# Linear attention with a gated feed-forward on one Trainium2 core: keys and outputs turned by VectorE blocks and a round trip through HBM instead of by TensorE

## The chip, the core and the metric

The kernel runs on one core of a Trainium2 chip. The core has five engines with their own instruction queues: TensorE (PE; its weight loads are listed apart as PEld), VectorE (DVE), ScalarE (ACT), GpSimd (POOL) and SyncE (SP), which here issues nearly all DMAs. The metric is the device time of one execution, in microseconds (us).

## What is computed

`y` is a recurrent linear attention over 768 steps for 4 batches and 8 heads of 48; its output, seen as 3072 tokens of 384, goes through a gated feed-forward layer of width 1536. All is float32.

```python
for t in range(S):
    cur = np.einsum('bhd,bhe->bhde', u[None] * kt, vt)
    y[:, :, t] = np.einsum('bhd,bhde->bhe', rt, state + cur)
    state = wt[:, :, :, None] * state + np.einsum('bhd,bhe->bhde', kt, vt)
...
gate = 1.0 / (1.0 + np.exp(-(x @ w_gate)))
val = x @ w_val
return (gate * val @ w_out)
```

## The kernel before

The sequence is cut into 24 pieces of 128 steps, which the code numbers `q`: `q // 4` is the place in the sequence (0 to 5), `q % 4` the batch. The text calls them chunks. Four chunks with the same place in the sequence make a row of 512 tokens, `n = q // 4`, for the feed-forward layer. Its weights are split into 12 blocks `f` of 128 hidden units.

**The order of the work.** Row 0 and the attention of the first chunks are ordered by a small planner (`plan.run()`), which the change doesn't touch. What follows is a loop over rows 1 to 5 and their 12 blocks, 60 steps in all, in an order written out by hand. One step issues on PE: `gate` (9 matmuls of 128x512 into the bank `pg`), `value` (9 into `pu`), and `down` of the step before (9 into `po`). On the other engines follow `sigmoid` (ACT, reads `pg`, writes `sg`), `hidden` (DVE, reads `pu`, writes `sg`), `hidden_hi` (ACT, `hh`) and `hidden_lo` (DVE, `hl`). There is one bank `pg` and one bank `pu`.

**The attention in the loop.** A step has four slots, before `gate`, before `value`, before `down` and after it. The table `todo` holds, for each of the 240 slots, what else is issued there. The attention of chunk q is done at slot `time` of `visit` (7, 19, 31 and 43 in each row of 48 slots, so every 12 slots or three steps). Around it stand:

- `load_pin`, `load_tok` (SP): decay, keys and receptances by lanes (`pin`), and all three by tokens (`tok`), for chunk q + 2.
- `prepare(q + 1)`, a few slots ahead of the visit: `bonus1`, `bonus2` (POOL, products of `tok` into `bon`), `scan_k` and `prep_k` (DVE, a scan into `eg` and the product with the keys), `fade`; `turn_k` (PE, four transposes of 112x128 keys into the bank `turn`) and `take_k` (ACT, three copies to `kT`); `prep_r` (DVE, a scan and a product), `bonus3` (DVE, a sum over `bon`) and `bonus4` (POOL, into `at`).
- `both(q)` (PE): `carry` and `blend` of chunk q into the banks `py` and `pz`, `score` and `total` of chunk q + 1 into `pa`. `pz` is a tile of the tag `pu`, so it is the same bank as that of `value`. Two steps of this order go through a no-operation on SP (`relay`).
- `take_y` (ACT, two copies into `bon`), and on DVE `mask`, `middle`, `keep` of chunk q + 1.
- `turn_x` (PE, three transposes of `bon`, 128x128, into the bank `turn`), `take_x` (ACT) and `rest_x` (DVE), three slots after the visit: they write chunk q's part of the feed-forward's input `x`.

Tiles of one tag take turns in a fixed number of buffers. `bon` has two, so that of chunk q + 2 is the one of chunk q, and the first writer of the new tile waits for the last reader of the old one.

Of the kernel before, what the change touches and what calls it, by code (L numbers as in the profile page):

```python
# [21 lines left out]
P = 128  # L22
C = 128
# [30 lines left out]
WHEN = [0, 2, 3, 5, 6]  # L54
EARLY = [(0, 3, 4, 4), (11, 16, 16, 16), (23, 26, 28, 28), (35, 38, 40, 40)]
HC = C // 2
# [159 lines left out]
def tile_kernel(ctx: ExitStack, tc: tile.TileContext, dec: bass.AP, tok: bass.AP, wts: bass.AP, u: bass.AP, side: bass.AP, out: bass.AP):  # L216
# [90 lines left out]
    def load_pin(q):  # L307
        t = p2.tile([P, KW + 2 * NP * C], F32, tag="pin", name=f"pin{q}")
        for i, j in ((0, KW), (KW, KW + 2 * NP * C)) if q == 0 else ((0, KW + 2 * NP * C),):
            nc.sync.dma_start(t[:, i:j], dec[place(q)][:, i:j])  # L310
        pin[q] = t[:L]

# [87 lines left out]

    def take_k(q):
        kT[q] = p1.tile([P, NP * L], F32, tag="kT", name=f"kT{q}")
        if not swapped(q):
            nc.scalar.copy(kT[q], bank["k", q][:, :NP * L])
# [27 lines left out]
    def total(q, p, o, s):  # L432
        m = D if o or swapped(q) else 64
        return nc.tensor.matmul(  # L434
            bank["a", q][64 * o:64 * o + m, s, NP * HC + p * D:NP * HC + (p + 1) * D],
            lhsT=kT[q][rows(q, s, o), p * L + 64 * o:p * L + 64 * o + m], rhs=values(q, p, o, s),
            start=True, stop=True, skip_group_check=True)
# [123 lines left out]
    def take_x(q):  # L561
# [9 lines left out]
        nc.scalar.activation(to[:, :, spot(q)], bank["x", q], AF.Copy, accum_out=acc_x[:, q:q + 1])  # L571

# [73 lines left out]
    def check_bounds():  # L646
# [181 lines left out]

# [74 lines left out]
```

## Time and profile before

| | |
|---|---|
| time, median of 3 runs | 565.79 us (564.51 to 567.89) |
| the profiled execution: time, span of its instructions | 565.15 us, 563.3 us |
| PE busy (share of the span) | 546.7 us (97%) |
| DVE busy | 329.9 us (59%) |
| ACT busy | 213.6 us (38%) |
| POOL busy | 99.6 us (18%) |
| mean granted TensorE clock, as a share of full speed | 0.997 |

The span runs from the first to the last instruction; the time is 1.85 us longer, for what lies around it. A busy share is a mean over the whole execution: what bounds a stage is read from the waits in it.

### The profile page before, as it was taken

The page shows a single profiled execution, that of the slowest core. Times are in us where ns is not written, and L with a number is a line of the kernel's source. Part 1 is how long each engine was busy: PE and PEld are TensorE (multiplying, and loading weights), DVE is VectorE, ACT ScalarE, POOL GpSimd, SP SyncE. Part 2 cuts the span into 40 slices and gives each one's busy share as a digit, 9 for nine tenths or more (in the row PEclk, how much of TensorE's full clock was granted, in tenths as well). Part 3 has the DMA queues.
Part 4 walks back from the last instruction along what each step waited for, and adds up shares of the span by engine and source line. Part 5 has one row for each costly group of instructions (what it writes and reads, how often), then busy time and mean ns, then how long its engine had stood idle before and what let it go on. Part 6 is the DMA issues. An engine that isn't in the chain of part 4 may idle for free.

```text
span 563.3 us, 12542 instructions
## 1 busy us (share of the span) xinstructions
PE 546.7 (97%) x5487; PEld 451.0 (80%) x5487; DVE 329.9 (59%) x477; ACT 213.6 (38%) x428; POOL 99.6 (18%) x86
## 2 busy tenths in 40 slices
PE   8899899999999999999999999999999999999995
PEld 7788788868788888888888888888888888888883
DVE  5889999897775764664654654654654622321221
ACT  3759544634543333423323422323423232312111
POOL 4453302142022111120210210220320200000000
PEclk9999999999999999999999999999999999999998
DMA  8499123603122032122022122022122000100001
GB/s 318 147 390 420 76 77 128 263 0 113 51 94 101 0 101 99 57 100 99 2 99 100 56 100 99 1 100 97 60 99 99 2 1 1 57 1 1 1 1 62
DMA packets 11570, 51.73 MB, mean 92 GB/s; under 512 B 1393, under 2 KB 1778, under 8 KB 9970
## 3 DMA queue, kind: packets, MB, share of 16 engines
q1 hardware_dynamic: 9346, 46.90, 22.3%
q10 hardware_dynamic: 2160, 3.93, 1.8%
q8 instruction: 45, 0.74, 0.5%
q14 instruction: 19, 0.16, 0.1%
HBM read 46.11 MB, written 4.72 MB: 90 GB/s over the span
## 4 chain that ended last, share of the span: by engine, by line
PE 84%; DVE 5%; DMA 4%; ACT 3%; issue 2%; SPq 1%; POOL 0%; ACTq 0%; DVEq 0%; POOLq 0%
PE po L635 23%; PE pg L592 16%; PE pu L592 15%; PE pu L595 8%; PE pg L595 7%; DMA raw<-wts 4%; PE po L631 2%; PE py L442 2%; PE pa L428 2%; PE pu L589 2%; PE pg L589 2%; PE pk L394 1%; PE pa L434 1%; PE px L551 1%; PE py L448 1%
## 5 line engine op out<-in xcount | busy, mean ns | idle before, releaser
L612 DVE TENSOR_TENSOR sg<-pu,sg 128x512 f32<-128x512 f32 (+2 forms) x78 | 50.6, 649 | 137.5 <-PE pu L595 135.3
L635 PE MATMUL po<-hh,w 128*128 128x512 f32 x402 | 127.7, 399 | 0.4 <-ACT hh L616 0.4
L592 PE MATMUL pg<-x,w 128*128 128x512 f32 x402 | 105.3, 397 | 0.0
L592 PE MATMUL pu<-x,w 128*128 128x512 f32 x402 | 102.5, 390 | 0.0
L605 ACT ACTIVATE sg<-pg 128x512 f32<-128x512 f32 (+2 forms) x78 | 44.0, 564 | 141.2 <-PE pg L595 135.0
L616 ACT CAST hh<-sg 128x512 fp32r<-128x512 f32 x67 | 41.5, 620 | 135.9 <-DVE sg L612 135.9
L592 PEld LDWEIGHTS pu<-x,w 128*128 128x128 f32 x402 | 75.2, 188 | 15.5
L592 PEld LDWEIGHTS pg<-x,w 128*128 128x128 f32 x402 | 73.6, 188 | 16.1 <-issue 0.3
L635 PEld LDWEIGHTS po<-hh,w 128*128 128x128 f32 x402 | 72.9, 188 | 14.3 <-ACT hh L616 0.8
L635 PE MATMUL po<-hl,w 128*128 128x512 f32 x201 | 78.6, 391 | 0.5 <-DVE hl L620 0.5
L620 DVE TENSOR_TENSOR hl<-sg,hh 128x512 fp32r<-128x512 f32 x67 | 50.6, 756 | 41.7 <-ACT hh L616 41.7
L329 POOL TENSOR_TENSOR bon<-tok,ub 128x384 f32<-128x384 f32 x21 | 27.4, 1303 | 208.3 <-DMA tok<-tok 179.3
L595 PE MATMUL pu<-x,w 128*128 128x512 f32 x201 | 56.8, 391 | 0.0
L595 PE MATMUL pg<-x,w 128*128 128x512 f32 x201 | 56.5, 389 | 0.0
L350 POOL TENSOR_TENSOR at<-eye,a 128x512 f32<-128x512 f32 x24 | 33.1, 1380 | 131.1 <-DVE a L336 124.8
L635 PEld LDWEIGHTS po<-hl,w 128*128 128x128 f32 x201 | 37.8, 188 | 9.5 <-DVE hl L620 1.1
L595 PEld LDWEIGHTS pg<-x,w 128*128 128x128 f32 x201 | 37.7, 188 | 8.1
L595 PEld LDWEIGHTS pu<-x,w 128*128 128x128 f32 x201 | 37.7, 188 | 7.9
L357 DVE TENSOR_TENSOR_SCAN eg<-pin,ends 112x516 f32<-112x516 f32 x24 | 34.8, 1450 | 7.1 <-DMA pin<-dec 7.1
L518 DVE COPY_PREDICATED at<-after,pa 128x512 f32<-128x512 int32 x24 | 17.7, 737 | 31.0 <-PE pa L434 27.6
L332 POOL TENSOR_TENSOR bon<-bon,tok 128x384 f32<-128x384 f32 x21 | 32.4, 1543 | 1.6
L377 DVE TENSOR_TENSOR_SCAN eg<-pin,heads 112x516 f32<-112x516 f32 x24 | 29.4, 1226 | 0.0
(94 smaller groups left out, 672.3 us busy)
## 6 DMA issues: line engine op xcount, KB each, us to landing
pin<-dec SPq DMA_DIRECT2D x23, 772.0 KB, 4.6
raw<-wts SPq DMA_DIRECT2D x12, 1152.0 KB, 10.8
tok<-tok SPq DMA_DIRECT2D x21, 576.0 KB, 5.8
y<-o ACTq DMA_DIRECT2D x15, 256.0 KB, 2.0
y<-o SPq DMA_DIRECT2D x3, 256.0 KB, 3.4
tok<-tok SPq DMA_DIRECT2D x3, 192.0 KB, 9.3
pin<-dec SPq DMA_DIRECT2D x1, 512.0 KB, 4.2
pin<-dec SPq DMA_DIRECT2D x1, 260.0 KB, 2.9
```

Source lines behind the costliest of these rows:

```text
L329: nc.gpsimd.tensor_tensor(out=bon[q], in0=tk[q][:, 0:DM], in1=ub, op=ALU.mult)
L332: nc.gpsimd.tensor_tensor(out=bon[q], in0=bon[q], in1=tk[q][:, DM:2 * DM], op=ALU.mult)
L350: engine.tensor_tensor(out=att[q], in0=eye.unsqueeze(1).unsqueeze(1).broadcast_to(shape), in1=a0, op=ALU.mult)
L357: nc.vector.tensor_tensor_scan(out=e[:, 516:0:-1], data0=t[:, 516:0:-1], data1=ends[:, 516:0:-1], initial=0.0, op0=ALU.mult, op1=ALU.add,)
L377: nc.vector.tensor_tensor_scan(out=e[:, WW:WW + 516], data0=t[:, 0:516], data1=heads[:, 0:516], initial=0.0, op0=ALU.mult, op1=ALU.add,)
L592: nc.tensor.matmul(t, lhsT=w[f][:, cols], rhs=x[n][:, a, k, spot], start=k == 0 and j == 0, stop=False)
L595: nc.tensor.matmul(t, lhsT=whi[f][:, cols], rhs=x[n][:, 1, k, i0 * C:i1 * C], start=False, stop=k == NKT - 1)
L605: nc.scalar.activation(sg, hid["g", n, f, i0], AF.Sigmoid)
L612: nc.vector.tensor_tensor(out=sg, in0=hid["u", n, f, i0], in1=sg, op=ALU.mult)
L616: nc.scalar.copy(hh, hid["s", n, f, i0])
L620: nc.vector.tensor_tensor(out=hl, in0=hid["s", n, f, i0], in1=hid["hi", n, f, i0].bitcast(F32), op=ALU.subtract)
L635: nc.tensor.matmul(to, lhsT=w[f][:, cols], rhs=h, start=first and i == 0, stop=last and i == 2, skip_group_check=True)
```

## The change

From chunk 10 on the keys are no longer turned by PE. DVE turns the 32x32 blocks of the key tile within themselves (`nc.vector.transpose` into `near`), one DMA writes the result to HBM (`far`), and four DMAs read it back, each into 32 partitions, in runs of 128 elements, so that the blocks come to their places. `take_k` then copies from `near` instead of from a PSUM bank. In the same way the outputs of the first three chunks of each row are turned: DVE blocks of `bon`, one write of 128x384, four reads in runs of 96 elements back into `bon`. The fourth chunk of a row is still turned by PE. `turn_k` moves to the slot of `prep_k`, eight slots before the visit, and `take_k` stays behind at three before; `turn_x` moves to the visit itself, `take_x` and `rest_x` to eight slots after it. `load_tok` is issued after the new DMAs. The tile `sg` has one buffer instead of two in the loop, to make room.

```diff
+AWAY = 10
...
-EARLY = [(0, 3, 4, 4), (11, 16, 16, 16), (23, 26, 28, 28), (35, 38, 40, 40)]
+EARLY = [(0, 3, 4, 4), (11, 11, 16, 16), (23, 23, 28, 28), (35, 35, 40, 40)]
+Q = 32
+NQ = P // Q
...
+    def away_k(q):
+        return q >= AWAY
+
+    def away_x(q):
+        return swapped(q) and q % B < B - 1
+
     def turn_k(q):
+        if away_k(q):
+            near = stage.tile([P, NP * C], F32, tag="blocks", name=f"bk{q}")
+            nc.vector.transpose(
+                out=near.rearrange("a (j p t) -> a p j t", j=NQ, t=Q),
+                in_=deep[q][:, KW:KW + NP * C].rearrange("a (p j t) -> a p j t", j=NQ, t=Q))
+            far = away.tile([P, NP * C], F32, tag="k", name=f"far_k{q}")
+            nc.sync.dma_start(far, near)
+            of = far.rearrange("(i t) (j w) -> t i j w", t=Q, j=NQ)
+            for j in range(NQ):
+                nc.sync.dma_start(near[j * Q:(j + 1) * Q].rearrange("a (i w) -> a i w", i=NQ), of[:, :, j])
+            bank["k", q] = near
+            return
...
     def take_k(q):
-        kT[q] = p1.tile([P, NP * L], F32, tag="kT", name=f"kT{q}")
+        kT[q] = p1.tile([P, NP * C], F32, tag="kT", name=f"kT{q}")
+        if away_k(q):
+            to = kT[q].rearrange("a (p o i t) -> a o i p t", p=NP, o=2, t=Q)
+            of = bank["k", q].rearrange("a (o i p t) -> a o i p t", o=2, i=2, t=Q)
+            nc.scalar.copy(to[:, 0], of[:, 0])
+            for s, half in enumerate(HALVES):
+                nc.scalar.copy(to[half, 1], of[HALVES[1 - s], 1])
+            return
...
     def turn_x(q):
+        if away_x(q):
+            near = stage.tile([P, NP * C], F32, tag="blocks", name=f"bx{q}")[:, :DM]
+            nc.vector.transpose(
+                out=near.rearrange("a (g k t) -> a k g t", g=NQ, t=Q),
+                in_=bon[q].rearrange("a (k g t) -> a k g t", g=NQ, t=Q))
+            far = away.tile([P, DM], F32, tag="x", name=f"far_x{q}")
+            nc.sync.dma_start(far, near)
...
+            for g in range(NQ):
+                nc.sync.dma_start(to[g * Q:(g + 1) * Q], of[:, :, g])
...
+            return
...
-        sg = hid["s", n, f, i0] = stage.tile([P, (i1 - i0) * C], F32, tag="sg", bufs=2, name=f"sg{n}_{i0}_{f}")
+        sg = hid["s", n, f, i0] = stage.tile([P, (i1 - i0) * C], F32, tag="sg", bufs=1 + (n < R0), name=f"sg{n}_{i0}_{f}")
...
         at(early, prep_k, q)
+        if away_k(q):
+            at(early, turn_k, q)
         at(early, fade, q)
-        at(turn, turn_k, q)
-        at(turn, take_k, q)
+        if away_k(q):
+            at(late, take_k, q)
+        else:
+            at(turn, turn_k, q)
+            at(turn, take_k, q)
...
-            prepare(q + 1, *EARLY[q - start] if q < start + B else (time - 7, time - 5, time - 3, time - 3))
+            prepare(q + 1, *EARLY[q - start] if q < start + B else (time - 8, time - 8, time - 3, time - 3))
         at(time, both, q)
         at(time, take_y, q)
         if q + 1 < NG:
+            at(time, mask, q + 1)
+        if q + 2 < NG:
+            at(time, load_pin, q + 2)
+        if away_x(q):
+            at(time, turn_x, q)
+        if q + 1 < NG:
             settle(q + 1, time)
         if q + 2 < NG:
-            at(time, load, q + 2)
-        at(time + 3, turn_x, q)
-        at(time + 3, take_x, q)
-        at(time + 3, rest_x, q)
+            at(time, load_tok, q + 2)
+        if not away_x(q):
+            at(time + 3, turn_x, q)
+        wait = 8 if away_x(q) else 3
+        at(time + wait, take_x, q)
+        at(time + wait, rest_x, q)
```

The queue of SP around the visit of chunk 13, which loads for chunk 15, before (`pin` and `tok` are the two loads; the number behind a name is its chunk, then the tile's own):

```order
L310 DMA pin14_2788<-dec 128x1544
L316 DMA tok14_2790<-tok 128x1152
L310 DMA pin15_3009<-dec 128x1544
L316 DMA tok15_3011<-tok 128x1152
L310 DMA pin16_3229<-dec 128x1544
```

And now, from the loads of chunk 15 to the next:

```order
L314 DMA pin15_3037<-dec 128x1544
L584 DMA far_x13_3041<-bx13_3039 128x384
L588 DMA bon13_2627<-far_x13_3041 32x4x96 x4
L320 DMA tok15_3052<-tok 128x1152
L408 DMA far_k15_3099<-bk15_3097 128x512
L411 DMA bk15_3097<-far_k15_3099 32x4x128 x4
L314 DMA pin16_3264<-dec 128x1544
```

Between the two loads of a visit stand the write and the four reads of chunk 13's output, and behind them the write and the four reads of chunk 15's keys.

The queue of DVE from the first step after that visit to `hidden` of the third, before (`x` is `rest_x`, `eg` and `pin` are `scan_k` and `prep_k`, then `prep_r`, `a0` is `bonus3`, `sg` is `hidden`, `hl` is `hidden_lo`):

```order
L581 TENSOR_TENSOR x3_2823<-px13_3040,x3_2823 128x3x128
L357 SCALAR_TENSOR_TENSOR eg15_3058<-pin15_3009,ends_77 112x516
L361 RECIPROCAL heads_80<-eg15_3058 112x4
L366 TENSOR_TENSOR pin15_3009<-pin15_3009,eg15_3058 112x512
L372 TENSOR_TENSOR ready15_3062<-state3_105,eg15_3058 112x192
L612 TENSOR_TENSOR sg2_0_6_3074<-pu2_0_6_3076,sg2_0_6_3074 128x512
L620 TENSOR_TENSOR hl2_0_6_3089<-sg2_0_6_3074,hh2_0_6_3087 128x512
L377 SCALAR_TENSOR_TENSOR eg15_3058<-pin15_3009,heads_80 112x516
L382 TENSOR_TENSOR pin15_3009<-pin15_3009,eg15_3058 112x512
L336 TENSOR_REDUCE a015_3111<-bon15_3055 128x8
L612 TENSOR_TENSOR sg2_0_7_3125<-pu2_0_7_3127,sg2_0_7_3125 128x512
```

And now:

```order
L361 SCALAR_TENSOR_TENSOR eg15_3093<-pin15_3037,ends_79 112x516
L365 RECIPROCAL heads_82<-eg15_3093 112x4
L370 TENSOR_TENSOR pin15_3037<-pin15_3037,eg15_3093 112x512
L404 STREAM_TRANSPOSE bk15_3097<-pin15_3037 128x4x4x32
L376 TENSOR_TENSOR ready15_3105<-state3_107,eg15_3093 112x192
L658 TENSOR_TENSOR sg2_0_6_3117<-pu2_0_6_3119,sg2_0_6_3117 128x512
L666 TENSOR_TENSOR hl2_0_6_3132<-sg2_0_6_3117,hh2_0_6_3130 128x512
L626 TENSOR_TENSOR x3_2915<-bon13_2627,x3_2915 128x3x128
L381 SCALAR_TENSOR_TENSOR eg15_3093<-pin15_3037,heads_82 112x516
L386 TENSOR_TENSOR pin15_3037<-pin15_3037,eg15_3093 112x512
L340 TENSOR_REDUCE a015_3151<-bon15_3090 128x8
L658 TENSOR_TENSOR sg2_0_7_3165<-pu2_0_7_3167,sg2_0_7_3165 128x512
```

`rest_x` of chunk 13 has moved from ahead of `scan_k` to behind the second step's `hidden_lo`, and a block transpose of the keys stands behind `prep_k`. The block transpose of chunk 13's output stands ahead of these rows, at the visit, behind `mask`.

The queue of POOL with the semaphores that each instruction waits for, before (`bon` is `bonus1` and `bonus2`, `at` is `bonus4`; each DMAHW name is one of the semaphores of the DMAs):

```order
L329 TENSOR_TENSOR bon14_2835<-tok14_2790,ub_89 128x384 [waits DMAHW2_49,PE_49,Activation_49]
L332 TENSOR_TENSOR bon14_2835<-bon14_2835,tok14_2790 128x384 [waits Pool_49]
L350 TENSOR_TENSOR at14_2893<-eye_84,a014_2891 128x512 [waits DVE_49]
L329 TENSOR_TENSOR bon15_3055<-tok15_3011,ub_89 128x384 [waits DMAHW4_49,PE_49,Activation_49]
L332 TENSOR_TENSOR bon15_3055<-bon15_3055,tok15_3011 128x384 [waits Pool_49]
```

And now:

```order
L333 TENSOR_TENSOR bon14_2862<-tok14_2824,ub_91 128x384 [waits DMAHW2_49,DMAHW6_49,DMAHW1_49,DMAHW7_49,DMAHW0_49,DVE_49]
L336 TENSOR_TENSOR bon14_2862<-bon14_2862,tok14_2824 128x384 [waits Pool_49]
L354 TENSOR_TENSOR at14_2926<-eye_86,a014_2924 128x512 [waits DVE_49,PE_49]
L333 TENSOR_TENSOR bon15_3090<-tok15_3052,ub_91 128x384 [waits DMAHW4_49,DMAHW5_49,DMAHW3_49,DMAHW6_49,DMAHW2_49,DVE_49]
L336 TENSOR_TENSOR bon15_3090<-bon15_3090,tok15_3052 128x384 [waits Pool_49]
```

`bonus1` of chunk 15 waited for PE, which read `bon` of chunk 13 last, in its transposes. It now waits for DVE, whose `rest_x` of chunk 13 reads that buffer last, eight slots after the visit.

## Rows read from the trace of the kernel before

**Rows 1.** Busy time of each engine in a stretch of two rows of tokens:

```profile
242.00:327.00 85.00, 85.00 (x864) 70.20 (x863) 48.18 (x76) 28.29 (x63) 15.98 (x12) 1.00 0.21 74
```

**Rows 2.** Waits of PE from 142 to 560 us: in total, times, longest:

```profile
PE pz L442 <- DVE sg L612: 0.9, 1, 0.9
```

**Rows 3.** Timeline of PE around chunk 13's visit: start, duration, engine, line, instruction:

```profile
259.48 0.25 PE L442 MATMUL py<-mid,pin 48*64 48x48 f32 x1
...
264.92 0.85 PE L595 MATMUL pu<-x,w 128*128 128x512 f32 x3
...
267.81 0.39 PE L635 MATMUL po<-hl,w 128*128 128x512 f32 x1
268.03 1.53 PE L592 MATMUL pg<-x,w 128*128 128x512 f32 x6
...
274.61 1.53 PE L592 MATMUL pg<-x,w 128*128 128x512 f32 x6
...
278.02 0.84 PE L595 MATMUL pu<-x,w 128*128 128x512 f32 x3
...
280.51 0.39 PE L635 MATMUL po<-hl,w 128*128 128x512 f32 x1
```

**Rows 4.** Timeline of PE, two starts of a step without attention:

```profile
505.28 1.52 PE L592 MATMUL pg<-x,w 128*128 128x512 f32 x6
511.40 1.52 PE L592 MATMUL pg<-x,w 128*128 128x512 f32 x6
```

**Rows 5.** Groups of instructions by line and shape: busy us, mean ns of one:

```profile
L394 PE MATMUL pk<-ident,pin 112*128 112x112 f32 x96 | 13.9, 268 | 0.8 <-ACT whole L571 0.7
...
L551 PE MATMUL px<-ident,bon 128*128 128x128 f32 x72 | 11.8, 273 | 0.5 <-ACT a L407 0.5
```

**Rows 6.** Timeline of DVE after that visit:

```profile
267.87 0.55 DVE L581 TENSOR_TENSOR x<-px,x 128x384 fp32r<-128x384 f32 x1
...
276.26 0.55 DVE L336 TENSOR_REDUCE a<-bon 128x8 f32<-128x384 f32 x1
278.97 0.69 DVE L612 TENSOR_TENSOR sg<-pu,sg 128x512 f32<-128x512 f32 x1 [2.16 <-PE pu L595]
```

**Rows 7.** Instructions of tiles `pin`, `tok`, 230 to 470 us: ns minimum/median/maximum:

```profile
L382 DVE TENSOR_TENSOR pin<-pin,eg x11: 691/693/694, 233.0 to 446.4; 112x512 f32<-112x512 f32 x11
...
L357 DVE TENSOR_TENSOR_SCAN eg<-pin,ends x10: 1222/1580/1939, 247.0 to 439.0; 112x516 f32<-112x516 f32 x10
L366 DVE TENSOR_TENSOR pin<-pin,eg x10: 661/1224/1229, 248.4 to 441.1; 112x512 f32<-112x512 f32 x10
...
L329 POOL TENSOR_TENSOR bon<-tok,ub x10: 1012/1028/1917, 247.1 to 438.9; 128x384 f32<-128x384 f32 x10
L332 POOL TENSOR_TENSOR bon<-bon,tok x10: 1342/1816/1824, 249.1 to 440.0; 128x384 f32<-128x384 f32 x10
```

**Rows 8.** DMA issues: line, KB each, median us from issue to landing:

```profile
pin<-dec SPq DMA_DIRECT2D x23, 772.0 KB, 4.6
...
y<-o ACTq DMA_DIRECT2D x15, 256.0 KB, 2.0
...
weigh<-side SPq DMA_DIRECT2D x1, 3.5 KB, 1.7
```

**Rows 9.** Timeline of SP at that visit:

```profile
260.80 0.33 SPq L310 DMA_DIRECT2D pin<-dec  x1
```

**Rows 10.** Timeline of ACT after that visit:

```profile
267.13 0.48 ACT L571 ACTIVATE x<-px 128x384 fp32r<-128x384 f32 x1
...
273.13 0.62 ACT L616 CAST hh<-sg 128x512 fp32r<-128x512 f32 x1 [2.19 <-DVE sg L612]
...
274.03 0.64 ACT L412 COPY kT<-pk 64x192 f32<-64x192 f32 x2
...
276.92 0.60 ACT L605 ACTIVATE sg<-pg 128x512 f32<-128x512 f32 x1 [2.25 <-PE pg L595]
```

**Rows 11.** Groups of instructions of DVE from 142 to 230 us (`w_lo`):

```profile
L299 DVE TENSOR_TENSOR w<-raw,w 128x1152 fp32r<-128x1152 f32 x5 | 7.5, 1491 | 0.0
```

More of the change, by code (lines that the diff above doesn't have):

```diff
@@ L223, in tile_kernel @@
     ps1 = own.enter_context(tc.tile_pool(name="ps1", bufs=1, space=PSUM))
+    away = own.enter_context(tc.tile_pool(name="away", bufs=2, space=bass.MemoryType.DRAM))
     early = tc.tile_pool(name="early", bufs=1)
@@ L299, in w_lo @@
         nc.vector.tensor_tensor(out=wlo[f], in0=full(f), in1=whi[f].bitcast(F32), op=ALU.subtract)
-    pin, tk, eg, bon, kT, att, ready, mid, bank = {}, {}, {}, {}, {}, {}, {}, {}, {}
+    deep, pin, tk, eg, bon, kT, att, ready, mid, bank = {}, {}, {}, {}, {}, {}, {}, {}, {}, {}
     def place(q):
@@ L310, in load_pin @@
             nc.sync.dma_start(t[:, i:j], dec[place(q)][:, i:j])
-        pin[q] = t[:L]
+        pin[q], deep[q] = t[:L], t
     def load_tok(q):
@@ L401, in take_k @@
     def take_k(q):
-        kT[q] = p1.tile([P, NP * L], F32, tag="kT", name=f"kT{q}")
+        kT[q] = p1.tile([P, NP * C], F32, tag="kT", name=f"kT{q}")
[6 more added lines that the diff above has]
+            return
         if not swapped(q):
-            nc.scalar.copy(kT[q], bank["k", q][:, :NP * L])
+            nc.scalar.copy(kT[q][:, :NP * L], bank["k", q][:, :NP * L])
             if q in LANES:
@@ L432, in total @@
     def total(q, p, o, s):
-        m = D if o or swapped(q) else 64
+        m, i = D if o or swapped(q) else 64, p * (C if away_k(q) else L) + 64 * o
         return nc.tensor.matmul(
             bank["a", q][64 * o:64 * o + m, s, NP * HC + p * D:NP * HC + (p + 1) * D],
-            lhsT=kT[q][rows(q, s, o), p * L + 64 * o:p * L + 64 * o + m], rhs=values(q, p, o, s),
+            lhsT=kT[q][rows(q, s, o), i:i + m], rhs=values(q, p, o, s),
             start=True, stop=True, skip_group_check=True)
@@ L548, in turn_x @@
     def turn_x(q):
+        if away_x(q):
[5 more added lines that the diff above has]
+            nc.sync.dma_start(far, near)
+            to = bon[q].rearrange("a (i w) -> a i w", i=NQ)
+            of = far.rearrange("(i f) (g w) -> f i g w", f=Q, g=NQ)
+            for g in range(NQ):
+                nc.sync.dma_start(to[g * Q:(g + 1) * Q], of[:, :, g])
+            bank["x", q] = to.rearrange("a i (k t) -> a k i t", t=Q)
+            return
         px = bank["x", q] = att_bank(f"px{q}")[:, :DM].rearrange("a (k c) -> a k c", c=C)
@@ L570, in take_x, with like @@
             to = x[n][:, 0]
-        nc.scalar.activation(to[:, :, spot(q)], bank["x", q], AF.Copy, accum_out=acc_x[:, q:q + 1])
+        nc.scalar.activation(like(q, to[:, :, spot(q)]), bank["x", q], AF.Copy, accum_out=acc_x[:, q:q + 1])
+    def like(q, t):
+        return t.rearrange("a k (i t) -> a k i t", t=Q) if away_x(q) else t
     def part_x(q):
@@ L580, in rest_x @@
         of = whole[0][:, :, spot(q)] if plain(q) else bank["x", q]
-        nc.vector.tensor_tensor(out=x[n][:, 1, :, spot(q)], in0=of, in1=x[n][:, 0, :, spot(q)].bitcast(F32), op=ALU.subtract)
+        nc.vector.tensor_tensor(
+            out=like(q, x[n][:, 1, :, spot(q)]), in0=of, in1=like(q, x[n][:, 0, :, spot(q)]).bitcast(F32), op=ALU.subtract)
     def up(s, side, n, f, i0, i1, e):
@@ L650, in check_bounds @@
         nc.vector.tensor_scalar(out=fine[:, 3, :NFF], in0=acc_t, scalar1=0.0, scalar2=None, op0=ALU.is_equal)
-        p1.tile([P, 72], F32, name="margin")
+        p1.tile([P, 8], F32, name="margin")
         count = p1.tile([P, 1], F32, name="count")
@@ L779, in both @@
         sums(q + 1, theirs)
-    def load(q):
-        load_pin(q)
-        load_tok(q)
     todo = {}
@@ L803, in settle @@
     def settle(q, time):
-        at(time, mask, q)
         at(time, middle, q)
@@ L814, in tile_kernel @@
     at(3, section1, start)
+    at(3, mask, start)
     settle(start, 3)
```

## The prediction

> **What bounds the kernel now.** I read the busy time by stretches first. In the loop PE is busy for all 85 us of a stretch of 85 us, at a granted clock of 1.00, the 2.4 GHz level; DVE is busy for 48 us of them, ACT for 28, POOL for 16 [rows 1]. A busy PE alone proves little, since its matmuls overlap and their ends are modelled. So next come its waits: from 142 to 560 us PE waited for another engine once, 0.9 us, when a first matmul into `pz` waited for `hidden` to have read that bank [rows 2]. PE's instruction stream thus sets the loop's time, and the one place where another engine can reach into it is that bank. The timeline of PE around chunk 13's visit then tells what a transpose costs in the stream.
>
> **What is removed.** A step without attention takes 511.40 - 505.28 = 6.12 us [rows 4]. The step with the four key transposes runs from 268.03 to 274.61, 6.58 us [rows 3]: they cost 0.46. For the three output transposes I compare two stretches between the same instructions, from the second half of `value` to the last matmul of `down`: 264.92 to 267.81 with them, 2.89 us, and 278.02 to 280.51 without, 2.49 [rows 3]. They cost 0.40. Chunks 10 to 23 lose the first, 14 x 0.46 = 6.4 us, and three chunks in each of four rows the second, 12 x 0.40 = 4.8 us. Together 11.2 us. PE has no idle time that could swallow this.
>
> The busy time of these instructions says otherwise: 0.268 us for a key transpose and 0.273 for an output transpose on average [rows 5], so 56 x 0.268 + 36 x 0.273 = 24.8 us. The steps' starts decide, since overlapped matmuls are counted twice in busy time.
>
> **What is added, and what hides it.** I count from the visit's start, 259.48 [rows 3]. In the changed kernel a period is 0.86 us shorter. `down`'s last matmul ahead of the next visit started at 280.51 and took 0.39 [rows 3], so the next visit begins 21.4 us after this one, and 20.6 in the changed kernel. By then `hidden` of the third step must have read the bank `pu`, or PE stands still in front of `pz`. By itself `hidden` ends at 278.97 + 0.69 [rows 6], 20.2 after the visit and 19.3 in the changed kernel. Two new chains reach it.
>
> *The keys' chain.* `scan_k` takes the place that `rest_x` had, 267.87 [rows 6], so 8.4. The scan takes 1.22 to 1.94 us and the product 0.66 to 1.22 [rows 7]; the long values come with POOL's `bonus1` and `bonus2` beside them, which now stand later, so I take the short ones and end at 10.4. No row shows a block transpose. It is a pass over 128x512 with one operand; a pass over 128x384 takes 0.55 [rows 6], and the scan's 1.22 is the upper bound; I take 0.6, to 11.0. The write of 256 KB has the shape of the outputs' write, which lands after 2.0 us [rows 8]; the upper bound is the 4.6 of a load of three times the size. To 13.0. Four reads of 64 KB are issued 0.33 us apart, as SP's other DMAs [rows 9], and the last lands between 1.7 (3.5 KB) and 4.6 us (772 KB) after its issue [rows 8]; I take 2.3, nearer to the small one, and 0.2 for the handovers. They have landed at 16.5. Behind them on ACT stands `take_k`, whose three copies ended at 274.67 where `hidden_hi` before them had ended at 273.75, 0.9 us [rows 10], and behind it `sigmoid` of the third step, 0.60 [rows 10], for which `hidden` waits, 0.69 [rows 6]. With handovers `hidden` ends at 18.9, inside 19.3: nothing is lost, and there is room of 1.7 us up to 20.6. ACT's wait for the reads itself costs nothing, since ACT had 2.25 us of idle time in front of that `sigmoid` [rows 10].
>
> *The bonus chain.* `bonus1` of chunk q + 2 now waits for `rest_x` of chunk q. `take_x` can start when `hidden_hi` of the second step is through, 273.13 + 0.62 [rows 10], less 0.40 for the transposes taken out: 13.9. `rest_x` starts 0.74 after `take_x` (267.13 to 267.87) and takes 0.55 [rows 6, 10]: 15.2. `bonus1` takes 1.03 (up to 1.92) and `bonus2` 1.82 (from 1.34) [rows 7]: 18.0. On DVE `bonus3`, 0.55, waits for them, and behind it `hidden`, 0.69 [rows 6]: 19.3, and 20.2 with the long `bonus1`. `prep_r` lies between, 1.22 and 0.69 [rows 7], and has from 15.2 to 18.0. So this chain too ends just in time, with 1.3 us of room, 0.4 at the long end.
>
> *The other additions.* The output's round trip has from about 4 us after the visit to 13.9; by the keys' prices it needs 6, and where its write has to stand behind the load of `pin`, issued at 260.80 [rows 9] and landed 4.6 later [rows 8], some 8 or 9. Hidden, and POOL and ACT would first feel it. `load_tok` goes out behind those reads, at about 8.5, and lands by 13 with the price of `pin`, ahead of `bonus1` at 15.2. `load_pin` keeps its place on SP, ahead of the new DMAs, so `scan_k` finds its data. The no-operations on SP that PE waits for stand behind the last read, which is issued at 14.2, six us before the next visit. 26 block transposes are 16 us on DVE, which idles 37 us in each stretch of 85 [rows 1]. The single `sg`: the next `sigmoid`, 276.92, starts 3.2 us after `hidden_hi` ended, 273.75 [rows 10], and `hidden_lo` of some 0.7 fits in between. PE loses no work that would bring idle time in, so the clock stays.
>
> *The first row.* `w_lo` stands on DVE twice in each of the visits of chunks 8 and 9, 1.49 us each [rows 11], once ahead of `scan_k` and once ahead of `rest_x`. The bonus chain then ends at 20.8, 0.2 late, at the long end 1.1. I take 0.25 a visit, 0.5 in all (0 to 2.2).
>
> **The sum.** The profiled execution took 565.15 us; 565.15 - 11.2 + 0.5 = 554.4. The median of the runs, 565.79, lies 0.6 above it, so the forecast is 555.0 us. 0.5% is 2.8 us, about what a measurement of this kernel can tell from no change.
>
> **The rivals.**
>
> *The chains miss by a little.* If the keys land 2.2 us later than 16.5, or POOL and DVE hold each other up by more than the rows show (a DVE pass beside POOL's grew from 0.66 to 1.22 [rows 7]), each of 14 visits loses some 0.5 us in front of `pz`: 7 us, 562. For it speaks that the keys' write is issued while `tok` may still be landing. Chance 0.17.
>
> *The round trip is long, and the kernel slower.* The place is the same, `pz` behind `hidden` behind `sigmoid` behind `take_k` behind the last read. Break-even is a stall of 11.2 / 14 = 0.8 us a visit, that is reads landed at 19.0 instead of 16.5, a trip of 8.0 us instead of 5.5. If both legs took the 4.6 us of a load, the trip would be 10.3, the stall 3.1 a visit, 43 us in all, and the time 598. Against it: the write's shape is in the trace, at 2.0 us. Chance 0.10. The Trainium skill ("VectorE: DVE Perf Modes", "Rules for kernel authors") advises TensorE for a full 128x128 transpose where PSUM will do as destination, which is the kernel before; no run here shows the other path yet, and that PE is this kernel's only engine without idle time [rows 1] is why I don't follow it.
>
> *PE is freed, but nothing comes of it.* The loop's pace could pass to the chain of `sigmoid`, `hidden` and `hidden_lo`, now with one `sg`, so that the time stays at 565. The 2 us and more of idle time in front of ACT's and DVE's instructions [rows 6, 10] speak against it. Chance 0.07.
>
> *The whole busy time comes back.* 24.8 us less, 541. The overlap in [rows 3] speaks against it; chance 0.04. The Trainium skill ("TensorE: Matmul & The Clock Gate", "Part 4: PE-mode transpose") gives about 275 ns for such a transpose in a kernel's context; the trace agrees with that as a duration, but not as a cost in the stream.
>
> **How the numbers follow.** Forecast 0.62, with a range of its own of 552.5 to 557.5 (no stall in the first row and a dearer transpose below, 2.2 us of stalls above). Of the small miss two thirds are still faster than 563. Faster: 0.62 + 0.04 + 0.12 = 0.78; same: 0.05 + 0.06 = 0.11; slower: 0.10 + 0.01 = 0.11. The range reaches over the small miss, 552 to 565; below it lies the busy-time case, above it the long trip.
>
> **What the profile after will show.** Right: no `pk` from chunk 10 on, `px` for four of the loop's sixteen chunks, visits 0.86 us closer together, write and last read of the keys landing within 6 us, `take_k` waiting on ACT for a DMA, and few waits of PE at `pz`. Wrong: a row in PE's waits of `pz` for DVE's `hidden` with 10 or more occurrences. If ACT's wait for the reads stands behind it, the keys' trip was mis-sized; if DVE's `bonus3` waiting for POOL does, the bonus chain was.

## The result and the profile after

The changed kernel takes 561.04 us (median of 20 runs, 558.79 to 565.31), the kernel before in the same session 565.88 (20 runs, 564.05 to 570.85). The ratio is 0.9909, interval 0.9887 to 0.9932: faster by 4.8 us, where 10.8 was forecast. The time lies inside the range given, near the price of the rival "the chains miss by a little", 562.

The profiled execution of the changed kernel took 565.31 us and hides part of this, for a reason ahead of the loop. Here is its busy time by stretches, the planner's part and the two rows of tokens of [rows 1]:

```profile
14.00:28.00 14.00, 11.57 (x195) 10.63 (x194) 9.14 (x12) 7.83 (x15) 3.85 (x3) 0.63 0.39 144
242.00:327.00 85.00, 83.86 (x898) 69.42 (x892) 52.05 (x84) 30.23 (x65) 17.02 (x12) 1.00 0.35 114
```

From 14 to 28 us, in work that the change doesn't touch, the granted clock was 0.63 on average: read in steps of 2 us, PE was busy for only 0.23 us from 14 to 16, and from 18 to 26 the clock stood at 0.50, the 1.2 GHz level. In the execution of the kernel before PE was busy for all of 14 to 16, and the clock was 1.00 throughout. Chunk 8's visit, the first that the change reaches, began at 155.46 instead of 151.32. Ahead of the loop all kernels below do the same, yet this start moves between 149.5 and 155.5 us. So beside each median I give the time from chunk 8's visit to chunk 23's, read as the starts of `py`'s first matmul; between them lies every transpose that the change removes. First the kernel before, then the changed one:

```profile
151.32 0.31 PE L442 MATMUL py<-mid,pin 48*64 48x48 f32 x2
...
472.42 0.26 PE L442 MATMUL py<-mid,pin 48*64 48x48 f32 x2
```

```profile
155.46 0.31 PE L471 MATMUL py<-mid,pin 48*64 48x48 f32 x2
...
471.99 0.26 PE L471 MATMUL py<-mid,pin 48*64 48x48 f32 x2
```

They stand 321.10 us apart before and 316.53 after. The loop gained 4.57, about the 4.8 of the medians.

What the change does is there. The groups of instructions by line and shape, which answer to [rows 5]:

```profile
L404 DVE STREAM_TRANSPOSE bk<-pin 128x512 f32<-128x512 f32 x14 | 10.0, 712 | 0.5
L416 PE MATMUL pk<-ident,pin 112*128 112x112 f32 x40 | 6.9, 306 | 0.7 <-ACT whole L613 0.7
L580 DVE STREAM_TRANSPOSE bx<-bon 128x384 f32<-128x384 f32 x12 | 6.7, 560 | 0.0
L593 PE MATMUL px<-ident,bon 128*128 128x128 f32 x36 | 6.3, 285 | 0.0
```

PE has 56 key transposes and 36 output transposes fewer, and DVE 14 and 12 block transposes more. But the second row of the windows above is short of PE work: 83.86 us of 85, where [rows 1] had 85.00. PE's waits from 142 to 560 us, against [rows 2]:

```profile
PE pz L471 <- DVE sg L658: 4.6, 7, 1.1
```

The forecast named this row as the sign of being wrong, from 10 occurrences on; there are 7. One of them, 0.9 us at chunk 8's visit, is the one of [rows 2]; all kernels below have it, with 0.4 to 1.1. The row counts idle time only. Measured from `py`'s first matmul of a visit to `pz`'s first, which follows 0.01 us later in an undisturbed visit, the new stalls are 0.50, 0.50, 1.46, 0.26, 1.45, 0.35, 1.18 and 0.52 us. They stand at the visits that follow those of chunks 8, 9, 11, 13, 15, 17, 18 and 19, and I number them by these, in whose periods they arise: 6.2 us in all. Chunk 18 shows how one comes about. Timeline of all engines from its visit (367.00) to the next:

```profile
377.80 0.71 DVE L404 STREAM_TRANSPOSE bk<-pin 128x512 f32<-128x512 f32 x1
378.12 0.38 SPq L320 DMA_DIRECT2D tok<-tok  x1
...
378.60 0.38 SPq L408 DMA_DIRECT2D far_k<-bk  x1
...
382.98 1.74 SPq L411 DMA_DIRECT2D bk<-far_k  x4
...
385.82 0.55 DVE L340 TENSOR_REDUCE a<-bon 128x8 f32<-128x384 f32 x1 [0.90 <-POOL bon L336]
...
386.39 0.41 ACT L428 COPY kT<-bk 128x256 f32<-128x256 f32 x1 [4.64 <-DMA bk<-far_k]
...
386.82 0.82 ACT L430 COPY kT<-bk 64x256 f32<-64x256 f32 x2
...
387.67 0.60 ACT L651 ACTIVATE sg<-pg 128x512 f32<-128x512 f32 x1
...
387.86 0.31 PE L471 MATMUL py<-mid,pin 48*64 48x48 f32 x2
388.29 0.69 DVE L658 TENSOR_TENSOR sg<-pu,sg 128x512 f32<-128x512 f32 x1 [1.92 <-ACT sg L651]
...
389.04 0.25 PE L471 MATMUL pz<-mid,pin 48*64 48x48 f32 x1 [0.86 <-DVE sg L658]
```

Read it from below. `pz` waits for `hidden`, `hidden` for `sigmoid`, `sigmoid` stands on ACT behind `take_k`, and `take_k` waited 4.64 us for the reads. `bonus3` ended at 386.37, 1.9 us ahead of that `hidden`: the bonus chain is not what ends last. The write went out 0.48 us behind `tok`'s load of 576 KB, and the reads follow it 4.4 us later; its median from issue to landing is 2.0 (last column, behind the KB each):

```profile
tok<-tok SPq DMA_DIRECT2D x21, 576.0 KB, 4.3
...
far_k<-bk SPq DMA_DIRECT2D x14, 256.0 KB, 2.0
bk<-far_k SPq DMA_DIRECT2D x56, 64.0 KB, 2.0
```

The largest stall, 1.46 after chunk 11's visit (219.15), has other company. DMA issues and `take_k` there, from the timeline:

```profile
231.80 0.33 SPq L408 DMA_DIRECT2D far_k<-bk  x1
...
234.00 0.37 ACTq L690 DMA_DIRECT2D y<-o  x1
234.02 1.83 SPq L411 DMA_DIRECT2D bk<-far_k  x4
...
235.03 0.34 ACTq L690 DMA_DIRECT2D y<-o  x1
...
236.03 0.34 ACTq L690 DMA_DIRECT2D y<-o  x1
...
238.91 0.41 ACT L428 COPY kT<-bk 128x256 f32<-128x256 f32 x1 [2.92 <-DMA bk<-far_k]
```

The writes of the row that leaves, 3 x 256 KB, run beside the reads; from the first read's issue to `take_k` it took 4.9 us.

### The profile page after: what moved, and what is told of

Its sections match the earlier page's. It is cut to its first block, busy times and chain, and to the rows that moved or that the text cites. A ratio compares the mean times of both kernels' runs of the same rounds, so it can differ in the third digit from the quotient of the medians.

```text
span 563.5 us, 12729 instructions
## 1 busy us (share of the span) xinstructions
PE 541.9 (96%) x5395; PEld 448.0 (80%) x5395; DVE 339.4 (60%) x503; ACT 218.9 (39%) x428; POOL 105.4 (19%) x86
## 4 chain that ended last, share of the span: by engine, by line
PE 69%; DVE 10%; DMA 8%; ACT 5%; issue 2%; POOL 2%; SPq 1%; ACTq 0%; DVEq 0%
PE po L681 17%; PE pg L638 13%; PE pu L638 13%; PE pu L641 6%; PE pg L641 6%; DMA pin<-dec 3%; DVE sg L658 2%; DMA bk<-far_k 2%; PE po L677 2%; PE pa L457 2%; DMA raw<-wts 2%; DVE w L303 2%; PE py L477 2%; PE py L471 2%; PE pa L463 1%
## 5 line engine op out<-in xcount | busy, mean ns | idle before, releaser
L681 PE MATMUL po<-hh,w 128*128 128x512 f32 x402 | 124.8, 392 | 0.0
L333 POOL TENSOR_TENSOR bon<-tok,ub 128x384 f32<-128x384 f32 x21 | 38.3, 1822 | 273.2 <-DVE x L626 180.9
L681 PEld LDWEIGHTS po<-hh,w 128*128 128x128 f32 x402 | 74.9, 188 | 15.2
L666 DVE TENSOR_TENSOR hl<-sg,hh 128x512 fp32r<-128x512 f32 x67 | 47.6, 711 | 41.7 <-ACT hh L662 41.7
L354 POOL TENSOR_TENSOR at<-eye,a 128x512 f32<-128x512 f32 x24 | 30.1, 1255 | 63.8 <-DVE a L340 55.7
L361 DVE TENSOR_TENSOR_SCAN eg<-pin,ends 112x516 f32<-112x516 f32 x24 | 30.7, 1278 | 8.3 <-DMA pin<-dec 5.7
L336 POOL TENSOR_TENSOR bon<-bon,tok 128x384 f32<-128x384 f32 x21 | 29.2, 1392 | 1.6
```

The costliest lines, as they stand in the source:

```text
L333: nc.gpsimd.tensor_tensor(out=bon[q], in0=tk[q][:, 0:DM], in1=ub, op=ALU.mult)
L336: nc.gpsimd.tensor_tensor(out=bon[q], in0=bon[q], in1=tk[q][:, DM:2 * DM], op=ALU.mult)
L354: engine.tensor_tensor(out=att[q], in0=eye.unsqueeze(1).unsqueeze(1).broadcast_to(shape), in1=a0, op=ALU.mult)
L361: nc.vector.tensor_tensor_scan(out=e[:, 516:0:-1], data0=t[:, 516:0:-1], data1=ends[:, 516:0:-1], initial=0.0, op0=ALU.mult, op1=ALU.add,)
L666: nc.vector.tensor_tensor(out=hl, in0=hid["s", n, f, i0], in1=hid["hi", n, f, i0].bitcast(F32), op=ALU.subtract)
L681: nc.tensor.matmul(to, lhsT=w[f][:, cols], rhs=h, start=first and i == 0, stop=last and i == 2, skip_group_check=True)
```

## The experiments

Theory K: all the freed PE time arrives, and the loss is the keys' chain, late reads ahead of `sigmoid` on ACT. Rival B: the bonus chain holds the bank. Rival T: the transposes freed less than counted. When K stood, a second question followed: why the reads are late, because of other transfers beside them (C) or by themselves (D). "Loop" is the stretch between the two visits in the profiled execution, with its difference to the 321.10 of the kernel before. The ratio and its interval are estimated from all the runs; they are not the quotient of the two medians.

| kernel | median | before, same session | ratio (interval) | loop |
|---|---|---|---|---|
| changed kernel | 561.04 | 565.88 | 0.9909 (0.9887 to 0.9932) | 316.53, -4.57 |
| `take_k` later | 556.19 | 565.21 | 0.9868 (0.9823 to 0.9913) | 311.40, -9.70 |
| outputs only, first form | 615.13 | 565.21 | 1.0885 (1.0844 to 1.0925) | |
| keys only | 571.55 | 565.21 | 1.0100 (1.0068 to 1.0133) | 325.56, +4.46 |
| `take_k` and `bonus3` later | 554.27 | 565.21 | 0.9806 (0.9780 to 0.9832) | 310.22, -10.88 |
| outputs only | 562.43 | 565.85 | 0.9942 (0.9908 to 0.9976) | 316.02, -5.08 |
| keys only, `take_k` later | 559.48 | 565.85 | 0.9888 (0.9856 to 0.9920) | 315.39, -5.71 |
| one read of four | 559.06 | 565.85 | 0.9855 (0.9820 to 0.9890) | 312.14, -8.96 |
| `bonus3` later | 559.75 | 565.85 | 0.9888 (0.9855 to 0.9920) | 316.31, -4.79 |
| `tok` first | 560.19 | 565.72 | 0.9908 (0.9878 to 0.9938) | 315.86, -5.24 |
| `y` later | 561.71 | 565.72 | 0.9916 (0.9889 to 0.9943) | 319.47, -1.63 |
| `tok` first and `y` later | 555.74 | 565.72 | 0.9842 (0.9801 to 0.9883) | 311.88, -9.22 |

**`take_k` one slot later**, behind the third step's `sigmoid`:

```diff
-            at(late, take_k, q)
+            at(late + 1, take_k, q)
```

> The changed kernel with take_k one slot later, so that on ScalarE sigmoid of the third step stands ahead of the copies that wait for the reads. Theory K (the keys' reads land late, and hold up take_k, sigmoid and hidden, for which pz waits): the waits at pz fall from some 6 us to 1.5 or less, those of the first row's two visits remain, and the time comes to 556 to 557.5, a ratio of 0.983 to 0.985. Rival B (bonus1 and bonus2 after rest_x, and bonus3 in front of hidden, set it): pz waits as before, 561. Rival T (the freed TensorE time was overestimated): few waits at pz, but the time stays at 560 to 561.

Measured 556.19. Only the first row's two stalls are left (0.50 and 0.49). The reads come no earlier; chunk 18's visit began at 358.39 here, and the timeline shows the new order:

```profile
374.44 1.74 SPq L411 DMA_DIRECT2D bk<-far_k  x4
...
374.95 0.60 ACT L651 ACTIVATE sg<-pg 128x512 f32<-128x512 f32 x1 [2.14 <-PE pg L641]
...
377.35 0.68 DVE L658 TENSOR_TENSOR sg<-pu,sg 128x512 f32<-128x512 f32 x1
...
377.87 0.41 ACT L428 COPY kT<-bk 128x256 f32<-128x256 f32 x1 [2.31 <-DMA bk<-far_k]
```

`take_k` starts 19.5 us after the visit, later than in the changed kernel (19.4), but `hidden` has gone ahead of it and PE doesn't stall. K holds: the lateness alone costs nothing here, the place of `take_k` on ACT does.

**Outputs only, and keys only.** For the first `AWAY` is 24 instead of 10, so that no key goes through HBM; for the second:

```diff
     def away_x(q):
-        return swapped(q) and q % B < B - 1
+        return False
```

> The changed kernel with all keys turned by TensorE again; only the outputs of three chunks a row go through HBM. Theory K: 12 x 0.40 = 4.8 us less than before, given back only in the first row's visits (the bonus chain, some 1 us): 561.5 to 562.5, a ratio of 0.992 to 0.994, and no waits at pz after the first row. Rival B: the waits at pz of the changed kernel's visits all remain, 5 us or more, and the time is that of before, 565 to 567.

> The changed kernel with all outputs turned by TensorE again; only the keys go through HBM. Theory K: 14 x 0.46 = 6.4 us are freed, and the waits at pz remain in most visits, some 0.3 to 1.4 us each, above all in those in which a row's output leaves: 562 to 565. Rival B: without the late bonus chain the waits at pz go, and the time is 559 to 560, better than the whole change.

Neither came out as expected. In the first the keys' transposes had gone, with the changed table of slots, to eight slots ahead of the visit, right behind `prep_k`, and PE stood in front of them. Its waits:

```profile
PE pk L416 <- issue: 36.1, 14, 3.4
PE pz L471 <- DVE sg L658: 0.9, 1, 0.9
```

That is not the undoing I meant. Keys only is 6.3 us slower than the kernel before. Its row at `pz`:

```profile
PE pz L471 <- DVE sg L658: 8.6, 8, 1.6
```

There is no late bonus chain in this kernel (`bonus2` ends 10 to 13 us after the visit), and the waits nearly doubled, so B falls. `bonus1` and `bonus2` now run beside `scan_k` and `prep_k`, and the block transpose ends 12.5 to 12.6 us after a visit that had no stall instead of 11.2.

**`take_k` later, and `bonus3` and `bonus4` two slots later:**

```diff
-        at(more, bonus3, q)
-        at(more, bonus4, q)
+        at(more + 2, bonus3, q)
+        at(more + 2, bonus4, q)
```

> take_k one slot later and bonus3 and bonus4 two slots later, so that neither new chain stands in front of hidden of the third step. Theory K: no waits at pz but those of the kernel before, all of the 11.2 us stay: 554.5 to 556, a ratio of 0.980 to 0.983. Rival B: the same time, but the first experiment would then have brought little. Rival T: 559 or more, with no waits at pz.

554.27, the fastest kernel of the study. No visit after chunk 8's has a stall. PE's starts, as above:

```profile
153.19 0.31 PE L471 MATMUL py<-mid,pin 48*64 48x48 f32 x2
...
463.41 0.26 PE L471 MATMUL py<-mid,pin 48*64 48x48 f32 x2
```

310.22 us, 10.88 less than before, 0.3 of it at chunk 8's visit: near the sum's 11.2, and T falls. Against the changed kernel it is 6.31 less, the 6.2 us of stalls.

**The parts again, undone cleanly.** Outputs only with PE's key transposes at their old slots, five ahead of the visit (`AWAY` is 24 again, and `EARLY` has the second numbers of the kernel before), and keys only with `take_k` one slot later:

```diff
-            prepare(q + 1, *EARLY[q - start] if q < start + B else (time - 8, time - 8, time - 3, time - 3))
+            prepare(q + 1, *EARLY[q - start] if q < start + B else (time - 8, time - 5, time - 3, time - 3))
```

> The first x-only kernel also stood the keys' transposes where TensorE had to wait for `prep_k`. Here the three outputs of a row go through HBM, the keys are turned by TensorE in the steps where the kernel before turns them, and `take_k` stands behind them as before. Theory K (what is given back comes from the keys' late reads alone): 4.8 us are taken out, about 0.9 are lost in the first row, so some 4 us less than the kernel before, 561 to 562, and no wait of TensorE in front of `pz` in the later rows. Rival B (the bonus chain, made late by the outputs' trip, holds the bank): waits in front of `pz` in every visit where the output goes through HBM, and 563 or more. Rival T (a transpose taken out frees less than 0.13 us each): no waits and 563 or more.

> The keys alone go through HBM, and ScalarE's `take_k` stands one step later, behind the third step's `sigmoid`. The same kernel with `take_k` ahead of that `sigmoid` was 6 us slower than the kernel before. Theory K: the loss there was this coupling alone, so the waits in front of `pz` go and the 6.4 us of the keys' transposes come out, 558 to 560; a late `kT` may still hold TensorE at the first matmul that reads it if it lands after the next visit's start by more than that matmul's distance. Rival (the keys' trip costs something else as well, such as its waits on SP in front of `pin`): 563 or more.

562.43, a little above K's range, and 559.48, inside it, both without a stall behind chunk 8's visit. I had expected the first row's stalls of the outputs. There `hidden` ends 22.07 us after chunk 8's visit, no earlier than in the changed kernel (22.09), but with the keys' transposes still in PE's stream the next visit follows at 22.12, not at 21.65. The loop gains 5.08 and 5.71, together 10.79, about the 10.88 of the whole. What made the keys alone 6 us slower than the kernel before was `take_k`'s place: with it one slot later they are 6 us faster, though their trips still take 5.4 to 8.4 us.

**One read of four** leaves out three quarters of the transposed keys:

```diff
-            for j in range(NQ):
+            for j in range(1):
```

> The changed kernel with one of the keys' four reads, so three quarters of the transposed keys are not read back (that part of the computation is left out). It sizes the reads: three issues of SP fewer, 0.46 us each in the trace, and less to land. Theory K: the keys land 1.4 to 2 us earlier, `take_k` no longer ends behind the third step's `value`, and of the 6.2 us of waits in front of `pz` 1 to 2 are left, nearly all in the first row; 556 to 557.5. Rival B: the waits stay at 5 us or more, 560 to 562.

Chunk 13's visit began at 260.61. From the timeline:

```profile
271.83 0.34 SPq L408 DMA_DIRECT2D far_k<-bk  x1
...
274.12 0.32 SPq L411 DMA_DIRECT2D bk<-far_k  x1
...
276.00 0.41 ACT L428 COPY kT<-bk 128x256 f32<-128x256 f32 x1 [0.97 <-DMA bk<-far_k]
```

`take_k` starts 1.88 us after the read's issue and 15.4 after the visit, against 18.2 with four reads. Three stalls of 0.5 are left, two of them in the first row. The median, 559.06, is above what I expected, but the loop gained 8.96; the profiled execution lost 4 us ahead of the loop as that of the changed kernel did (chunk 8 at 155.32).

**`bonus3` and `bonus4` alone later**, the diff above without `take_k`'s:

> The changed kernel with `bonus3` and `bonus4` alone two steps later, behind the third step's `hidden` on VectorE; `take_k` stays ahead of the third step's `sigmoid` on ScalarE. Theory K: only the first row's two waits can shrink, 4.5 to 6 us of waits in front of `pz` are left, 560 to 561. Rival B: the waits go, 555 to 557.

559.75, and 4.9 us of waits at `pz` stay, nearly all behind the first row. B falls a second time as the cause of the loss in the later rows.

**Why the reads are late.** Three kernels leave `take_k` where the change put it and move other transfers. In the first `load_tok` is issued right behind `load_pin`:

```diff
             at(time, load_pin, q + 2)
+            at(time, load_tok, q + 2)
...
-        if q + 2 < NG:
-            at(time, load_tok, q + 2)
```

In the second the writes of the leaving row are issued eight slots later:

```diff
+        if R0 <= n < NC_ - 1:
+            at((n + 1 - R0) * NFF * 4 + 10, send, n, o)
```

The third does both.

> In the changed kernel SP issues `tok`'s load of 576 KB behind the outputs' reads, 8.4 to 9.7 us after the visit, so that it is still landing when the keys' trip begins at 11.3. Here it stands right behind `pin`'s load, as in the kernel before. The trip from the end of the keys' block transpose to `take_k`'s start took 5.4 to 5.6 us in the visits of the keys-only kernel without other transfers beside it, and 5.4 to 7.9 in the changed kernel. Theory C (other transfers beside the keys' reads make the trip long): in the visits of chunks 10, 13, 14, 17, 18, 20 the trip falls to 5.4 to 5.8, the waits in front of `pz` at chunks 13, 17, 18 go, those of the first row (1.0) and of chunks 11, 15 and 19 (some 3.4) stay; from chunk 8's visit to chunk 23's some 2 us less than the 316.5 of the changed kernel; 558.5 to 559.5. Rival D (the four reads need 7 us by themselves): no change of the trips, 561.

> In the changed kernel three writes `y<-o` of 256 KB go out on ScalarE's queue at the time of the keys' reads in the visits of chunks 11, 15 and 19. Here they are issued two steps later, behind the next visit; nothing else is moved. Theory C: in these visits the trip falls from 7.1 us to 5.5, `take_k` starts at 18.1 instead of 19.7, their waits in front of `pz` of 1.46, 1.45 and 0.52 go or fall to 0.1, and from chunk 8's visit to chunk 23's it takes some 3 us less than 316.5; 557 to 558.5. Rival D: trips and waits stay, 561.

> Both: `tok` is loaded right behind `pin`, and the writes `y<-o` go out behind the next visit; `take_k` keeps its place ahead of the third step's `sigmoid`. Theory C: the trips are 5.4 to 5.8 us in all visits, as the forecast had it, only the first row's 1.0 us of waits are left, and from chunk 8's visit to chunk 23's it takes 311 to 312 us, 9 to 10 less than the 321.1 of the kernel before; 555.5 to 557. Rival D: 5 us or more of waits stay, 560 to 561.

The trip from the end of the keys' block transpose to `take_k`'s start in the period after each chunk's visit, and behind the stroke the stall at `pz` at its end (0 stands for under 0.02), in us, worked out from the timelines. The first row (5.5 to 5.8 in all four, stalls 0.5) is left out:

| chunk | changed kernel | `tok` first | `y` later | both |
|---|---|---|---|---|
| 10 | 6.1 / 0 | 6.0 / 0 | 6.3 / 0 | 6.3 / 0 |
| 11 | 7.1 / 1.46 | 7.0 / 1.27 | 5.5 / 0 | 5.6 / 0.10 |
| 12 | 5.5 / 0 | 5.4 / 0 | 7.7 / 1.02 | 5.6 / 0 |
| 13 | 7.0 / 0.26 | 6.6 / 0 | 6.7 / 0 | 7.0 / 0.28 |
| 14 | 6.1 / 0 | 5.6 / 0 | 6.0 / 0 | 5.7 / 0 |
| 15 | 7.1 / 1.45 | 7.6 / 1.88 | 5.4 / 0 | 5.6 / 0 |
| 16 | 5.4 / 0 | 5.3 / 0 | 9.6 / 2.93 | 5.3 / 0 |
| 17 | 7.0 / 0.35 | 5.5 / 0 | 5.4 / 0 | 5.4 / 0 |
| 18 | 7.9 / 1.18 | 5.7 / 0 | 8.2 / 1.45 | 5.5 / 0 |
| 19 | 6.3 / 0.52 | 6.9 / 1.38 | 5.5 / 0 | 5.5 / 0 |
| 20 | 6.1 / 0 | 5.5 / 0 | 7.9 / 1.15 | 5.6 / 0 |
| 21 | 5.4 / 0 | 5.3 / 0 | 5.9 / 0 | 5.3 / 0 |

`tok` first shortens the trips of chunks 14, 17, 18 and 20 as C says, less so those of 10 and 13, and leaves 11, 15 and 19. Its total was not as C had it: the loop is 0.7 us shorter than in the changed kernel where 2 were expected, and the median is 560.19 and not 558.5 to 559.5: the stalls of 15 and 19 grew to 1.88 and 1.38. `y` later brings 11, 15 and 19 down to 5.5, but its total, too, is not C's 557 to 558.5: the writes now fall into the next visit, ahead of the outputs' reads, `tok` and the keys, whose trips in the visits of chunks 12, 16 and 20 grew to 7.7 to 9.6. The worst stall, 2.93, is that behind chunk 16's visit (318.39); the period that begins with it took 24.89 us, over 4 above an undisturbed one. From the timeline:

```profile
325.56 1.34 ACTq L697 DMA_DIRECT2D y<-o  x3
325.82 2.03 SPq L588 DMA_DIRECT2D bon<-far_x  x4
...
327.90 0.46 SPq L320 DMA_DIRECT2D tok<-tok  x1
...
329.60 0.34 SPq L408 DMA_DIRECT2D far_k<-bk  x1
...
334.30 3.15 SPq L411 DMA_DIRECT2D bk<-far_k  x4
...
339.20 0.40 ACT L428 COPY kT<-bk 128x256 f32<-128x256 f32 x1 [6.39 <-DMA bk<-far_k]
```

With both moved, the visits from 14 on have trips of 5.3 to 5.7, and beside the first row's 0.99 us only 0.38 of stalls is left. Chunk 18 in that kernel, whose visit began at 358.41, against the changed kernel's above:

```profile
368.89 0.71 DVE L404 STREAM_TRANSPOSE bk<-pin 128x512 f32<-128x512 f32 x1
...
369.63 0.34 SPq L408 DMA_DIRECT2D far_k<-bk  x1
...
371.62 1.73 SPq L411 DMA_DIRECT2D bk<-far_k  x4
...
375.07 0.41 ACT L428 COPY kT<-bk 128x256 f32<-128x256 f32 x1 [2.24 <-DMA bk<-far_k]
```

The write lands in 2.0 us, not 4.4, and the trip is 5.5. The time is 555.74, the loop 9.22 us shorter than before. C holds for these visits, and D falls: the same reads take 5.3 to 5.7 where nothing stands beside them. Chunks 10 and 13 keep trips of 6.3 and 7.0 in this kernel; the account of the prediction below comes back to them. Which resource the transfers share (the DMA engines or HBM) these runs don't tell.

## Why the prediction was wrong

**Right: what is removed.** Forecast 11.2 us; without stalls the loop gained 10.88. The key transposes are worth a little less than 0.46: undisturbed periods fell from 21.33 to 20.54, 0.79 instead of 0.86. By that the 26 sets of transposes make 10.3 of the 10.88; 0.3 is the shorter wait at chunk 8's visit, and the rest came in the first row, whose two periods were longer than the others before (22.49 and 21.67). The other 14 us of busy time did not come back, so the starts of the steps were the right rows.

**Right: the place.** That `pz` behind `hidden` is the one point at which other engines reach PE, and the order `take_k`, `sigmoid`, `hidden` in front of it, is what the waits show.

**Right but for small sizes, in three visits of four: the keys' chain by itself.** The block transpose took 0.71 us (0.6 assumed) and ended at 11.2 (11.0); the write landed after 2.0. The reads were issued some 0.45 apart, not 0.33, and `take_k` took 1.26, not 0.9. Yet an undisturbed trip ends 5.3 to 5.7 after the transpose, where 16.5 - 11.0 = 5.5 was forecast. From `take_k`'s start to `hidden`'s end it is 2.6 us, so PE stalls once `take_k` starts later than 20.5 - 2.6 = 17.9 after the visit. Against 16.6 to 16.9 alone there was room of 1.0 to 1.3, not 1.7.

**Wrong in the fourth visit of each row: "`scan_k` takes the place that `rest_x` had", with the short values.** The fourth chunk of a row (11, 15, 19) is still turned by PE, and its `rest_x` stays three slots behind the visit, ahead of `scan_k`. The next `bonus1` need not wait for a late `rest_x` there, and `bonus1` and `bonus2` run beside the scan and the product as in the kernel before. After chunk 11's visit (219.15):

```profile
228.08 1.58 DVE L361 TENSOR_TENSOR_SCAN eg<-pin,ends 112x516 f32<-112x516 f32 x1
228.65 1.82 POOL L336 TENSOR_TENSOR bon<-bon,tok 128x384 f32<-128x384 f32 x1
...
229.80 1.23 DVE L370 TENSOR_TENSOR pin<-pin,eg 112x512 f32<-112x512 f32 x1
...
231.06 0.71 DVE L404 STREAM_TRANSPOSE bk<-pin 128x512 f32<-128x512 f32 x1
```

The scan took 1.58 us and the product 1.23, where 1.23 and 0.66 stand in chunk 18's visit, and the block transpose ended at 12.6, not 11.2. The next visit is due at 20.9 there, so `take_k` must start by 18.3, and a trip of 5.5 leaves a room of 0.2. With nearly the same trips, 7.0 and 7.1, chunk 17's visit was followed by a stall of 0.35 and chunk 11's by one of 1.46. The three stalls behind such visits are 3.4 of the 6.2 us; by these times it took both the late block transpose and the long trip. `y` later shows it for the trip: shortened to 5.5, it leaves no stall behind these visits. An earlier block transpose was not run.

**The step that failed: "They have landed at 16.5 ... nothing is lost."** Write and reads were priced by rows of transfers with nothing beside them, and the price was used for all 14 visits. Of the changed kernel's twelve visits in the table the trip is 5.4 or 5.5 in three, 6.1 to 7.9 in the others, and `hidden` came up to 1.46 us late. Two neighbours were in reach of the profile. The forecast had `load_tok` go out at about 8.5 and land by 13, while its write went out at 11: an overlap by its own numbers. With the outputs' trip in front `tok` went out at 8.4 to 11.1. And the writes of the leaving row were seen only as a row from which to price a write [rows 8], not as transfers in the same 3 us as the reads of chunks 11, 15 and 19. The rival "the chains miss by a little" was thus the case, with both of its reasons, `tok` and POOL beside DVE; the writes `y` it did not name. Its price of 7 us was 6.2 in fact, but from 8 visits of 0.26 to 1.46 and not from 14 of 0.5, so that the sums agree is partly luck. With both neighbours moved and `take_k` where the forecast had it, the kernel takes 555.74, against 555.0 forecast.

**The bonus chain** was forecast to end at 19.3 with `hidden`. With `take_k` out of the way `hidden` ended at 19.6 to 19.7 in the later rows, and it cost 0.50 in each of the first row's two visits (0.25 was taken; the sum was 0.5 and became 1.0).

**A third neighbour, seen in the traces and not tested.** In the kernel with both moved, chunks 10 and 13 still have trips of 6.3 and 7.0 with neither neighbour beside them. The profile counts DMA packets by queue, and beside the queues of the loads and writes named so far it has one that it calls `instruction`. Chunk 13's visit in that kernel began at 254.86, its reads at 268.16; this queue from 268 to 273 us, with packets, MB and the share of 16 DMA engines:

```profile
q8 instruction: 1, 0.02, 1.5%
```

That is one packet, in the trace one of 16 KB that took 1.17 us, in the middle of the reads. From 371 to 376, around chunk 18's reads with a trip of 5.5, this queue moved nothing. In the four kernels of the table such a packet lies between the first read's issue and `take_k` in nine of the listed visits: those of chunks 10 and 13 in all four, and that of chunk 16 with `y` later. There the stretch took 4.0 to 4.9 us; in the visits with neither such a packet nor the writes `y` beside the reads it took 3.3 to 3.8. In keys only the write of chunk 21 took 4.1 us, though SP had issued nothing in the 9 us before it, and a packet of this queue of 1.53 us lies in it. No run moves these packets, so that they are the cause is a reading of the traces and not shown by an experiment.

## What to carry to other kernels

A transfer's price from a quiet row is its lower end: before a round trip is put ahead of something that mustn't be late, list what else each queue issues in those microseconds, in every kind of visit, and price the trip with that beside it. The start of the trip, too, is to be read in every kind of visit, for the change itself can leave one of them as it was. Then ask what stands behind the waiting instruction on its engine. One slot later for `take_k`, behind the instruction that the bank needs, was worth 5 us (561.04 to 556.19) without making the transfers faster; moving the neighbouring transfers away was worth about the same (555.74).

## What was unexpected of the hardware

- A write of 256 KB landed in 2.0 us, and in 4.4 when a load of 576 KB had been issued 0.48 us ahead of it on the same queue; four reads of 64 KB behind it took 3.4 us from the first issue to the reader's start, and 4.9 with three writes of 256 KB beside them.
- One read of 64 KB in runs of 512 bytes was through after 1.9 us, four after 3.4: three more cost 1.5, about their issue time on SP (three times some 0.45).
- Block transposes on DVE took 0.71 us for 128x512 and 0.56 for 128x384, near the other passes of these sizes [rows 6].
- The same four reads took 4.0 to 4.9 us to the reader's start in the nine visits in which a 16 KB packet of the queue `instruction` lay among them, and 3.3 to 3.8 in those without it and without the writes; no run tests it.
